# A recurrent attention and a gated MLP on one core: weight signs on GpSimd as f32 words, and a new order of the whole program

## The chip, the core and the metric

The kernel runs on one core of a Trainium2 chip. A core has TensorE (PE, with its weight loads shown as PEld), VectorE (DVE), ScalarE (ACT), GpSimd (POOL) and SyncE (SP), which issues most DMAs. The engines run side by side, each through its own list of instructions in order, and wait for each other by semaphores. SBUF is the working memory of 128 partitions; PSUM, in eight banks, takes what TensorE computes.

The metric is device microseconds of one execution. Before the change the median of three runs is 501.91 us (501.64 to 502.25).

## The reference

For 4 batches, 8 heads, 768 steps and head size 48, a state of 48 x 48 a head is carried along:

```python
for t in range(S):
    cur = np.einsum('bhd,bhe->bhde', u[None] * kt, vt)
    y[:, :, t] = np.einsum('bhd,bhde->bhe', rt, state + cur)
    state = wt[:, :, :, None] * state + np.einsum('bhd,bhe->bhde', kt, vt)
```

The result, as x with 3072 tokens of 384, goes through an MLP with d_ff = 2048:

```python
h = x @ w_in
g = np.where(h >= 1, h, np.where(h <= -1, 0.0, (h + 1) ** 2 / 4))
return g @ w_out
```

The weights come as 64-bit floats, all else as 32-bit ones, and the result is 32-bit.

## The kernel before, in words

**Attention.** The sequence is cut into 12 segments u = 0..11 of 64 steps x 4 batches, 256 tokens each. In a segment VectorE scans w forward and backward (L550 and L545) for the decay products, scales k (L571) and r (L621) with them, and TensorE does the rest in 64 x 64 matmuls: `among` (L591) gives the scores of all pairs of steps, `picked` (L597) keeps the ones that count, `umat` (L660) the segment's own contribution to the state, `crossed` and `along` (L703) the output. k is also transposed (L630). For the first three segments (u < EARLY) the term with u is made by a second `among` on k scaled by u (`with_u`, L561, on ScalarE); later ones make it on VectorE and GpSimd (L609, L611, L614, L617).

**x.** The output y^T of a segment leaves PSUM as an operand x of the MLP, in two parts: a high part rounded for the fast matmul, and the low part that is left (`yevac`, L775 to L781). Each head has 48 rows of 64, so a last quarter of y is spread over the rows that are free: by matmuls with a permutation `perm` in segments 0 and 1 (L800, from a copy at L805), by DMAs from `last` after that. In the last two blocks (FLAT) y goes to `xf` unsplit and is split later, in `divided` (L1150, L1152).

**MLP.** Six blocks of 512 tokens (two segments each) pass 16 slices f of d_ff. `products` does one step (block, slice): nine matmuls into h (L1369), the gate on ScalarE and VectorE (L1178 to L1183), nine matmuls into three accumulators (L1389), two steps behind. Block 0 does slices 0 to 4 of each half alone, and block 1 slices 0 to 13, since a half is one segment and can begin sooner. The last three blocks (FAST) use a scheme with fewer products in the second half (L1045).

**Weights.** Each slice's 768 columns of w_in and w_out come as 64-bit floats, once, and are made into 32-bit ones in `weight(f)`. In order: a DMA into `wraw`; ScalarE takes the upper word with its exponent moved by 2^-112 into `fl` (L481); ScalarE puts the three bits of the lower word that an f32 still holds, as 16-bit numbers, into every other half word of `wraw` (L483); GpSimd, or VectorE for f in SIGNS, puts the sign, a 16-bit 0 or 32768, into the other halves (L485); VectorE shifts `fl` left by three and joins both (L487), so the f32 weight stands in `fl`. ScalarE, or VectorE for f in SPLITS, rounds it into the high part (L477, L475), and VectorE subtracts for the low part (L490). `fl` has three buffers.

**The order.** A planner (`Plan`) writes the order of all engines' instructions by hand. Each `op` has an engine, an estimated cost, a due time, and what it reads and writes; `order` simulates the engines and takes, whenever one is free, the ready operation with the most urgent key. `best` repeats this with keys from `late` (how long before the end an operation must run) and random shakes, and keeps the order with the shortest simulated end. `kept_warm` then puts multiplications of zeros (`zeros`, L439) into gaps of PE, so that its clock stays up.

At the start, SP's loads are ranked: w of both halves, rk of one half, the constants `cst`, rk of the other, weight 0, v, then the rest. `perm` is loaded too.

## Time and profile before

| | |
|---|---|
| median of three runs | 501.91 us (501.64 to 502.25) |
| the profiled execution | 503.06 us; its span, from the first to the last instruction, 501.5 us |
| busy: PE, PEld | 488.0 us (97%), 426.8 us (85%) |
| busy: DVE, ACT, POOL | 404.1 us (81%), 312.7 us (62%), 101.4 us (20%) |
| MLP products, L1369 and L1389 (three groups) | 220.1, 80.3 and 44.5 us of PE |
| zeros, L439 | 13.2 us of PE, all before 40 us |
| weights' signs, L485 on GpSimd | 13 instructions, 41.8 us |
| DMA | 54.30 MB, of it the permutation 192 KB, the constants 98 KB |

A row of a group names line, engine, operation, out<-in, shapes and count, then busy time in us, the mean ns of one, and the idle time of the engine before them with what ended it. A row of the timeline gives start and length in us. The busy time of PE includes the zeros. In the stages' rows the clock is the share of full speed that TensorE was granted.

### The profile page before, as it was taken

The page shows a single profiled execution, that of the slowest core. Times are in us where ns is not written, and L with a number is a line of the kernel's source. Part 1 is how long each engine was busy: PE and PEld are TensorE (multiplying, and loading weights), DVE is VectorE, ACT ScalarE, POOL GpSimd, SP SyncE. Part 2 cuts the span into 40 slices and gives each one's busy share as a digit, 9 for nine tenths or more (in the row PEclk, how much of TensorE's full clock was granted, in tenths as well). Part 3 has the DMA queues.
Part 4 walks back from the last instruction along what each step waited for, and adds up shares of the span by engine and source line. Part 5 has one row for each costly group of instructions (what it writes and reads, how often), then busy time and mean ns, then how long its engine had stood idle before and what let it go on. Part 6 is the DMA issues. An engine that isn't in the chain of part 4 may idle for free.

```text
span 501.5 us, 13736 instructions
## 1 busy us (share of the span) xinstructions
PE 488.0 (97%) x5767; PEld 426.8 (85%) x5767; DVE 404.1 (81%) x702; ACT 312.7 (62%) x658; POOL 101.4 (20%) x80
## 2 busy tenths in 40 slices
PE   6979999999999999999999999999999999999996
PEld 4768988889999998888888788889899989898985
DVE  5899999988888898898999878779877675675573
ACT  4669799855555473765555656788866565465461
POOL 1656604530111111303031124432100000000000
PEclk9989999999999999999999999999999999999999
DMA  8984750522343434446153212222141000010002
GB/s 293 400 300 163 300 211 17 185 81 86 107 133 107 141 103 138 169 137 215 39 210 105 106 52 74 42 52 55 30 118 22 1 1 1 23 41 1 3 1 69
DMA packets 33286, 54.30 MB, mean 108 GB/s; under 512 B 15424, under 2 KB 22720, under 8 KB 33216
## 3 DMA queue, kind: packets, MB, share of 16 engines
q1 hardware_dynamic: 32784, 52.95, 31.9%
q8 instruction: 47, 0.77, 0.6%
q10 hardware_dynamic: 432, 0.39, 0.2%
q14 instruction: 23, 0.19, 0.1%
HBM read 47.04 MB, written 4.72 MB: 103 GB/s over the span
## 4 chain that ended last, share of the span: by engine, by line
PE 90%; DVE 4%; DMA 2%; issue 2%; ACT 1%; SPq 0%; DVEq 0%; ACTq 0%
PE h L1369 39%; PE acc L1389 20%; PE acc L1045 10%; PE bank L1045 9%; PE bank L703 4%; PE bank L591 3%; PE bank L630 2%; PE bank L660 1%; DMA cst<-in_consts 1%; DMA rk<-in_rk 1%; DVE fl L487 1%; PE bank L439 1%; PE acc L591 1%; DVE wt L490 1%; DVE y L545 0%
## 5 line engine op out<-in xcount | busy, mean ns | idle before, releaser
L1369 PE MATMUL h<-x,wt 128*128 128x512 f32 (+1 forms) x1035 | 220.1, 360 | 3.0 <-DVE x L779 2.9
L1369 PEld LDWEIGHTS h<-x,wt 128*128 128x128 f32 x1035 | 169.5, 189 | 31.7 <-DVE x L779 3.1
L1389 PE MATMUL acc<-gh,wt 128*128 128x256 f32 (+1 forms) x402 | 80.3, 335 | 0.0
L1389 PEld LDWEIGHTS acc<-gh,wt 128*128 128x128 f32 x402 | 60.9, 188 | 7.4
L1007 DVE SCALAR_TENSOR_TENSOR rk<-rk,h 128x512 f32<-128x512 f32 x48 | 32.8, 683 | 35.8 <-ACT rk L1006 34.2
L1178 ACT ACTIVATE g<-h 128x256 f32<-128x256 f32 (+1 forms) x67 | 31.9, 476 | 44.8 <-PE h L1369 40.6
L1004 ACT ACTIVATE rk<-h 128x512 f32<-128x512 f32 x48 | 28.6, 596 | 38.8 <-PE h L1369 38.8
L485 POOL TENSOR_SCALAR wraw<-fl 128x768 uint16<-128x768 f32 x13 | 41.8, 3224 | 51.4 <-ACT wraw L483 49.9
L1180 DVE SCALAR_TENSOR_TENSOR g<-g,h 128x256 f32<-128x256 f32 (+1 forms) x67 | 35.2, 529 | 14.4 <-ACT g L1179 12.4
L1389 PE MATMUL acc<-gl,wt 128*128 128x256 f32 (+1 forms) x201 | 44.5, 329 | 0.0
L1182 ACT CAST gh<-g 128x256 fp32r<-128x256 f32 (+1 forms) x67 | 32.7, 494 | 18.8 <-DVE g L1180 8.8
L617 POOL TENSOR_TENSOR r<-cst,d 128x512 f32<-128x512 f32 x18 | 20.2, 1143 | 99.8 <-PE bank L703 81.7
L1183 DVE TENSOR_TENSOR gl<-g,gh 128x256 fp32r<-128x256 f32 (+1 forms) x67 | 38.7, 589 | 0.8 <-ACT gh L1182 0.7
L1389 PEld LDWEIGHTS acc<-gl,wt 128*128 128x128 f32 x201 | 32.3, 188 | 4.0
L1179 ACT ACTIVATE g<-g 128x256 f32<-128x256 f32 (+1 forms) x67 | 34.4, 513 | 1.1
L550 DVE TENSOR_TENSOR_SCAN p<-wq,seeds 128x520 f32<-128x520 f32 x24 | 32.0, 1331 | 3.2 <-DMA wq<-in_w 2.3
L1006 ACT ACTIVATE rk<-rk 128x512 f32<-128x512 f32 x48 | 30.4, 634 | 0.9
L545 DVE TENSOR_TENSOR_SCAN y<-wq,seeds 128x520 f32<-128x520 f32 x24 | 29.8, 1242 | 0.8
L609 POOL TENSOR_TENSOR nk<-nk 128x768 f32<-128x768 f32 x9 | 17.3, 1920 | 61.4 <-DMA nk<-in_nk 37.9
L1013 DVE TENSOR_TENSOR gl<-rk,gh 128x512 fp32r<-128x512 f32 x36 | 25.5, 717 | 2.7 <-ACT gh L1012 2.4
L1013 DVE TENSOR_TENSOR g_again<-rk,nk_again 128x512 fp32r<-128x512 f32 x33 | 22.8, 701 | 5.8 <-ACT nk_again L1012 5.5
L1012 ACT CAST gh<-rk 128x512 fp32r<-128x512 f32 x36 | 22.1, 619 | 8.3 <-DVE rk L1007 4.7
(212 smaller groups left out, 914.5 us busy)
## 6 DMA issues: line engine op xcount, KB each, us to landing
rk<-in_rk SPq DMA_DIRECT2D x24, 512.0 KB, 5.3
wraw<-in_wbits SPq DMA_DIRECT2D x16, 768.0 KB, 7.5
nk<-in_nk SPq DMA_DIRECT2D x9, 768.0 KB, 4.7
wq<-in_w SPq DMA_DIRECT2D x24, 260.5 KB, 2.9
vn<-in_v SPq DMA_DIRECT2D x12, 384.0 KB, 6.8
last<-in_w SPq DMA_DIRECT2D x12, 256.0 KB, 3.0
out_y<-xf SPq DMA_DIRECT2D x15, 128.0 KB, 1.8
out_y<-g SPq DMA_DIRECT2D x6, 256.0 KB, 2.2
```

The source lines that it names most:

```text
L485: op(on, 0.62 if f in SIGNS else 3.2, due, [("fl", k)], [("raw", f)], lambda: e.tensor_scalar(out=half(1), in0=s, scalar1=0.0, scalar2=327 ...
L550: V.tensor_tensor_scan(out=pv[:, q].rearrange("p n c -> p (n c)"), data0=w[:, 0:SEG], data1=sv, initial=0.0, op0=ALU.mult, op1=ALU.add,)
L1007: op("DVE", 0.66, due, [("h", n)], [qk], lambda: V.scalar_tensor_tensor(out=gf, in0=gf, scalar=1.0, in1=bank[plan.given[hk]], op0=ALU.min, ...
L1013: op("DVE", 0.67, due, [key, ("h", i, k)], fresh_in(("l", i, k)), lambda: V.tensor_tensor(out=spare(k, 3 + i), in0=x, in1=spare(k, i).bitc ...
L1045: PE.matmul(bank[i][:, half * UT : half * UT + UT], lhsT=w[wi], rhs=g[gi], start=(b, i) not in opened, stop=True, skip_group_check=True)
L1178: op("ACT", c, due, [("h", n)], [("g", gk)], lambda: nc.scalar.activation(gs, hs(), AF.Relu, scale=0.5, bias=0.5), uses=[hk])
L1179: op("ACT", c, due, (), [("g", gk)], lambda: nc.scalar.activation(gs, gs, AF.Square))
L1180: op("DVE", 0.13 + 0.53 * k, due, [("h", n)], [("g", gk)], lambda: nc.vector.scalar_tensor_tensor(out=gs, in0=gs, scalar=1.0, in1=hs(), op ...
L1182: op("ACT", c, due, [("g", gk)], [("gh", gk)], lambda: nc.scalar.copy(ghs, gs))
L1183: op("DVE", 0.17 + 0.54 * k, due, [("g", gk), ("gh", gk)], [("gl", gk)], lambda: nc.vector.tensor_tensor(out=gls, in0=gs, in1=ghs.bitcast( ...
L1369: nc.tensor.matmul(hp, lhsT=wx[f][:, cs], rhs=xt[:, j, :], start=n == 0, stop=n == 8)
L1389: nc.tensor.matmul(o[j], lhsT=wx[f][:, cs], rhs=gt, start=first and i == 0, stop=stop and i == 2, skip_group_check=True)
```

## The change

**Weights.** `xf[0]`, the unsplit x of even blocks, holds two tiles z of 768 words until block 2 needs it. GpSimd multiplies `fl` by 0.0 into z for every slice: what is left is a word with only the sign. ScalarE writes the low bits into the lower half of each word of z, and VectorE joins z with the shifted `fl`. SIGNS is gone, SPLITS is empty. For f of 4 and more, GpSimd copies the high part in ScalarE's place (SPARED); for the first four ScalarE does it. The copies of y into x of block 2 write z's names too, so that they wait for the last weight.

**x.** FLAT holds blocks 1 to 5 (it was 4 and 5): y of these is copied unsplit into `xf`, and `divided` splits it, for blocks 1 to 3 planned right behind their second segment.

**Start.** rk of both halves comes ahead of the constants; u stands in two new columns of w, so that `with_u` no longer reads `cst`; `perm` is made on GpSimd by a fill and three copies, and is no longer loaded; u's broadcast (`u_sb`) is loaded after weight 5.

**Planner.** It models PE's instruction stream in blocks of 256 with edges and fetch times, a price for the switch between small and wide matmuls, and holds PE up to 0.25 us for another small operation after a small one. Costs of PE's small operations are lower, the zeros' cost per column is higher (fewer columns in a gap). There are 12 shakes in place of 40, and then 19 listed moves, each of which shifts keys near one time. The result is another order of the whole program.

```diff
-FLAT = {NB - 2, NB - 1}
+FLAT = set(range(1, NB))
 
 WARM = 12
 
 SCRATCH = 2048
 
-USE, SPAN, COLUMN = 0.68, 3.4, 0.00168
+USE, SPAN, COLUMN = 0.68, 3.4, 0.00184
 
 EAGER, LATE = 16.0, 0.3
-RISES = 7.0
-COLD = 7.0
+RISES = COLD = 6.0
 
 LANES = 8
 
-BACK, SHAKES, SHAKE, SEED = 4, 40, 0.7, 5
+BACK, SHAKES, SHAKE, SEED = 4, 12, 0.7, 3
+
+MOVES = (521500, 587009, 625859, 75142, 354096, 937336, 551989, 701578, 29685, 79344, 78778, 524362, 665920, 756794, 334125, 534668, 621384, 343240, 480776)
...
-    BLOCK, FETCH = 256, 3.9
+    BLOCK, EDGE, LEAD, DENSE = 256, 194, 3, 1 / 700
+    FETCH, BUSY, SLOWER = 3.75, 45.0, 5.0
+    SWITCH, HOLD, LOOK = 0.125, 0.25, 30.0
+    EVENT = 0.00025
+    RATES, WAY = ((8.0, 300e3), (60.0, 390e3), (1e9, 280e3)), 2.1
...
+        for move in MOVES:
+            self.nudge(move)
...
+    def attempt(self, keys):
+
+        for op, key in zip(self.ops, keys):
+            op["key"] = key - self.LOOK * op["look"]
+        order = self.order()
+        if order is None:
+            return False
+        for _ in range(3):
+            was, self.put_in = self.put_in, self.idle(order)
+            self.replay(order)
+            if {n: x[-1] for n, x in was.items()} == {n: x[-1] for n, x in self.put_in.items()}:
+                break
+        end = max(self.end.values())
+        if self.found is None or end < self.found[0]:
+            self.found = end, order, (self.begin, self.end, self.given, self.extra, self.put_in, keys)
+            return True
+        self.put_in = self.found[2][-2]
+        return False
...
+    def nudge(self, move):
+
+        self.back()
+        draw = random.Random(move)
+        keys = self.late() if draw.random() < 0.1 else list(self.keys)
+        at, wide, much = draw.uniform(0.0, self.found[0]), draw.choice((4.0, 10.0, 25.0)), draw.choice((0.3, 1.0, 3.0, 8.0))
+        for n in range(len(keys)):
+            if abs(self.begin[n] - at) < wide:
+                keys[n] += draw.gauss(0.0, much)
+        return self.attempt(keys)
...
+    def pe_takes(self, n, t, pe, between=0.0):
+
+        op = self.ops[n]
+        idle = self.records(n)
+        was = pe["small"] and not idle
+        cost = op["cost"] + self.SWITCH * (op["small"] != was) + self.EVENT * op["code"]
+        for code, start, span in ((idle, between, t - between), (op["code"] * (1 + self.DENSE), t, cost)):
+            past = -(pe["count"] - self.EDGE) % self.BLOCK
+            if past < code:
+                at = start + span * past / code
+                when = pe["edge"] + (self.SLOWER if at < self.BUSY else self.FETCH)
+                if start == t:
+                    cost += max(0.0, when - at)
+                pe["edge"] = max(at, when)
+            pe["count"] += code
+        pe["small"] = op["small"]
+        return cost
...
+            if e == "PE" and pe["small"] and forced.get(e) is None:
+                n = min((n for n in open_[e] if ops[n]["small"] and ready(n) <= t + self.HOLD), key=lambda n: (ready(n), n), default=None)
+                if n is not None:
+                    t = max(t, ready(n))
...
-SPLITS = {2, 7}
-SIGNS = {9, 10, 12}
+SPLITS = set()
+SPARED = set(range(4, NF))
+SIGN, HALF = 1.0, 1.08
...
-    xf = tiles(len(FLAT), [128, 3, WIDE], F32, "xf")
+    xf = tiles(2, [128, 3, WIDE], F32, "xf")
...
-        def front():
-
-            return wraw[f].rearrange("p c two -> p (c two)")[:, 0:768]
-
-        def half(i):
-            return front().bitcast(U16).rearrange("p (c two) -> p c two", two=2)[:, :, i]
+        z = xf[0].rearrange("p a b -> p (a b)")[:, 768 * (f % 2) : 768 * (f % 2) + 768]
+        zk = ("z", f % 2)
+
+        def low_half():
+            return z.bitcast(U16).rearrange("p (c two) -> p c two", two=2)[:, :, 0]
 
...
-            if f in SPLITS:
+            if f in SPARED:
+                G.tensor_copy(w_hi[f], s)
+            elif f in SPLITS:
                 V.tensor_copy(w_hi[f], s)
             else:
                 A.copy(w_hi[f], s)
...
-        op("ACT", 1.09, due, (), [("raw", f)], lambda: A.activation(half(0), words(0, U32), AF.Copy, scale=LOW))
-        on, e = ("DVE", V) if f in SIGNS else ("POOL", G)
-        op(on, 0.62 if f in SIGNS else 3.2, due, [("fl", k)], [("raw", f)], lambda: e.tensor_scalar(
-            out=half(1), in0=s, scalar1=0.0, scalar2=32768.0, op0=ALU.is_lt, op1=ALU.mult))
-        op("DVE", 0.97, due, [("raw", f), ("flight", f % FLIGHT)], [("fl", k)], lambda: V.scalar_tensor_tensor(
-            out=s.bitcast(I32), in0=s.bitcast(I32), scalar=3, in1=front(), op0=ALU.logical_shift_left, op1=ALU.bitwise_or), port=True)
-        op(*(("DVE", 0.48) if f in SPLITS else ("ACT", 0.83)), due, [("fl", k)], [("wh", f), ("raw", f)], split, port=f in SPLITS)
+        op("POOL", SIGN, due, [("fl", k)], [zk], lambda: G.tensor_scalar(out=z, in0=s, scalar1=0.0, scalar2=None, op0=ALU.mult))
+        op("ACT", 1.09, due, [("raw", f), ("flight", f % FLIGHT)], [zk], lambda: A.activation(low_half(), words(0, U32), AF.Copy, scale=LOW))
+        op("DVE", 0.97, due, [zk], [("fl", k)], lambda: V.scalar_tensor_tensor(
+            out=s.bitcast(I32), in0=s.bitcast(I32), scalar=3, in1=z.bitcast(I32), op0=ALU.logical_shift_left, op1=ALU.bitwise_or), port=True)
+        op(*(("POOL", HALF) if f in SPARED else ("DVE", 0.48) if f in SPLITS else ("ACT", 0.83)), due, [("fl", k)], [("wh", f), ("raw", f)], split, port=f in SPLITS and f not in SPARED)
...
-            load(due, wq[slot[q]], a["w"][u, q], [("w", slot[q])], first=rank(1 - q))
-            load(due, rk[slot[q]], a["rk"][u, q], [("k", slot[q]), ("r", slot[q])], first=rank(4 - 2 * q))
+            s = slot[q]
+            load(due, wq[s], a["w"][u, q], [("w", s)], first=rank(1 - q))
+            load(due, rk[s], a["rk"][u, q], [("k", s), ("r", s)], first=rank(3 - q))
         if u == 0:
-            load(due, cst, a["consts"], ["cst"], first=3)
+            load(due, cst, a["consts"], ["cst"], first=4)
...
-            load(due, perm, a["perm"], ["perm"], [vk])
+            op("POOL", 0.4, due, [], ["perm"], lambda: G.memset(perm, 0.0))
+            for j in range(3):
+                def shifted(x, lo):
+                    return x.rearrange("p (h c) -> p h c", h=2)[:, :, lo : lo + 16]
+                op("POOL", 0.2, due, ["cst"], ["perm"], lambda j=j: G.tensor_copy(
+                    shifted(perm[:, 128 * j : 128 * j + 128], D), shifted(ident, 16 * j)))
...
-                A.mul(ku[:, q, cs], rk[slot[q]][:, 1, cs], u_col[:, 2 * q + pr : 2 * q + pr + 1])
+                A.mul(ku[:, q, cs], rk[slot[q]][:, 1, cs], wq[slot[q]][:, SEG + 1 + pr : SEG + 2 + pr])
...
-                op("ACT", 1.0, due, [("k", s), "cst"], [("ku", q), "nk"], lambda q=q: with_u(q))
+                op("ACT", 1.0, due, [("k", s), ("w", s)], [("ku", q), "nk"], lambda q=q: with_u(q))
...
-                op("ACT", 0.27 if what else 0.48, due, [("b", by[g])], [names(what, 0, g)], lambda g=g, w=what: yevac(g, 0, w))
+                op("ACT", 0.27 if what else 0.48, due, [("b", by[g])], [names(what, 0, g)] + [("z", i) for i in range(2) if blk == 2], lambda g=g, w=what: yevac(g, 0, w))
...
+                if u % 2 and u // 2 in FLAT and u // 2 < NB - 2:
+                    divided(u // 2)
...
-            if b + 1 in FLAT:
+            if b + 1 in FLAT and b + 1 >= NB - 2:
...
-    wz = np.pad(wz.reshape(NU, 2, 2, D, SEG), [(0, 0)] * 4 + [(0, 1)])
+    wz = np.pad(wz.reshape(NU, 2, 2, D, SEG), [(0, 0)] * 4 + [(0, 3)])
+    wz[..., SEG + 1 :] = u.reshape(2, 2, 2, D).transpose(0, 2, 3, 1)
```

More of the change, by code (lines that the diff above doesn't have):

```diff
@@ L86, in __init__, with add @@
         self.given, self.extra = {}, {}
-    def add(self, engine, cost, emit, due, reads=(), writes=(), port=False, size=0, fresh=True, first=None, grab=False, uses=(), drop=None, code=0):
+    def add(self, engine, cost, emit, due, reads=(), writes=(), port=False, size=0, fresh=True, first=None, grab=False, uses=(), drop=None, code=0, small=False, look=False):
         deps = {self.writer[x] for x in (*reads, *writes) if x in self.writer}
@@ new lines, in replay @@
+    def replay(self, order):
+        ops = self.ops
+        free, end, begin, lands = {}, {}, {}, []
+        port = bus = 0.0
+        pe = dict(count=self.LEAD, edge=-99.0, small=False)
+        for n in order:
+            op = ops[n]
+            e = op["e"]
+            t = max((end[m] + self.after(m, n) for m in op["deps"]), default=0.0)
+            if n in self.extra:
+                t = max(t, end[self.extra[n]] + self.HOPS[ops[self.extra[n]]["e"]])
+            t = max(t, free.get(e, 0.0))
+            if op["port"]:
+                t = max(t, port)
+            if op["size"] and len(lands) >= LANES:
+                t = max(t, lands[-LANES])
+            cost = op["cost"]
+            if e == "PE":
+                cost = self.pe_takes(n, t, pe, free.get(e, 0.0)) * (2 if t < RISES else 1)
+            begin[n], end[n] = t, t + cost
+            free[e] = end[n] - self.OVERLAP.get(e, 0.0)
+            if op["port"]:
+                port = free[e]
+            if op["size"]:
+                bus, end[n] = self.lands(bus, t, op["size"])
+                lands.append(end[n])
+        self.begin, self.end = begin, end
@@ L233, in order @@
         forced, given, extra = {}, {}, {}
[L234 to L241 removed]
+        pe = dict(count=self.LEAD, edge=-99.0, small=False)
         spare = [(0.0, b, None) for b in SPARE]
@@ L249, in ready @@
                 t = max(t, min(spare)[0]) if spare else never
-            if ops[n]["code"] > 64:
-                t = max(t, fetched(ops[n]["code"]) - ops[n]["cost"])
+            if ops[n]["small"]:
+                past = -(pe["count"] + self.records(n) - self.EDGE) % self.BLOCK
+                m, took = n, 0.0
+                while m is not None:
+                    code = ops[m]["code"] * (1 + self.DENSE)
+                    if past < code:
+                        when = pe["edge"] + (self.SLOWER if t < self.BUSY else self.FETCH)
+                        return max(t, when - took - ops[m]["cost"] * past / code)
+                    past, took, m = past - code, took + ops[m]["cost"], ops[m]["then"]
             return t
```

159 lines of the change are left out of this document (79 added, 80 removed).

## The prediction

> **What bounds the kernel now.** I read the page's head first, then the busy time by stage, then the chain of waits in the stage that loses time.
>
> ```profile
> span 501.5 us, 13736 instructions
> PE 488.0 (97%) x5767; PEld 426.8 (85%) x5767; DVE 404.1 (81%) x702; ACT 312.7 (62%) x658; POOL 101.4 (20%) x80
> ```
>
> ```profile
> 9.50:29.50 20.00, 17.00 (x312) 13.05 (x312) 17.86 (x26) 13.45 (x24) 10.79 (x4) 0.91 1.04 399
> ...
> 105.00:310.00 205.00, 205.00 (x3230) 178.16 (x3229) 178.14 (x318) 115.45 (x287) 40.08 (x33) 1.00 0.37 122
> 310.00:496.50 186.50, 186.10 (x1190) 167.62 (x1188) 131.48 (x243) 118.38 (x224) 15.48 (x20) 1.00 0.12 29
> ```
>
> The columns are the stretch, then busy time and count of PE, PEld, DVE, ACT and POOL, then the granted clock, DMA share and GB/s. TensorE is the bound: 97% of the span, and 205.00 of 205.00 us from 105 to 310, with 0.4 us missing in the 186.5 after that. The head of the kernel is different: PE counts as busy there for 17 of 20 us, but much of that work is not wanted by anyone. Its rows between the end of the first segment's attention and the first product say so:
>
> ```profile
> 18.96 1.11 PE L703 MATMUL bank<-r,vn 64*48 64x64 f32 x64
> 20.01 2.61 PE L439 MATMUL bank<-zero 128*128 128x512 f32 x8
> 22.45 1.53 PE L800 MATMUL bank<-ob,nk 128*128 128x128 f32 x12
> 23.82 2.25 PE L439 MATMUL bank<-zero 128*128 128x512 f32 x8
> ...
> 29.46 1.21 PE L1369 MATMUL h<-x,wt 128*128 128x256 f32 x8 [2.90 <-DVE x L779]
> 30.60 1.89 PE L591 MATMUL bank<-rk,nk 64*64 64x64 f32 x64
> ```
>
> L439 multiplies zeros to hold the clock. From 20.07 to 29.46 us, 9.39 us, PE does 1.53 us of work that counts (the spreading, L800) apart from a single matmul. The chain of waits tells what it waits for:
>
> ```profile
> 2.36 5.36 DMA cst<-in_consts
> ...
> 7.81 0.92 ACT nk L561 x2
> ...
> 13.31 1.53 PE bank L439 x6
> ...
> 26.93 0.94 DVE fl L487
> 27.87 0.47 DVE x L779
> 28.34 0.60 DVE rk L571
> 28.93 0.48 DVE x L779
> ```
>
> So x, the operand of the first product, is late because VectorE decodes a weight (L487) and scales another segment's k (L571) between and ahead of the two halves of x (L779). ScalarE does the same one step earlier: the copies that feed L800 wait behind a weight.
>
> ```profile
> 21.64 0.27 ACT L805 COPY ob<-bank 128x128 f32<-128x128 f32 x1
> 21.79 1.10 ACT L483 ACTIVATE wraw<-wraw 128x768 uint16<-128x768 uint32 x1
> 22.74 0.26 ACT L805 COPY ob<-bank 128x128 f32<-128x128 f32 x1
> 24.48 0.47 ACT L781 CAST x<-bank 128x384 fp32r<-128x384 f32 x1
> 25.66 0.46 ACT L781 CAST x<-bank 128x384 fp32r<-128x384 f32 x1
> ```
>
> The last instruction's chain runs on PE from there, so a microsecond won before 29.46 us is kept to the end, if the engines that feed PE can follow.
>
> **The change, part by part.** *What x needs.* Its own work after 20.07 us is two copies (0.27 + 0.26), the spreading (1.53), two casts (0.47 + 0.46), two subtractions (0.47 + 0.48), 3.94 us; five changes of engine at some 0.05 us, as between the chain's rows 28.93 + 0.48 and 29.46, make 4.2. Of 9.39 us, 5.2 are other work standing in the way. Ahead of it the change gives more: the scaling by u (L561) no longer waits for the constants, which landed at 7.72 us, but reads u beside w; that and the later fillers (1.53 us at 13.31) I take at 0.5, 0 to 2. The head can thus win 5.7 us, and 7.2 at most.
>
> *What the weights need.* The sign moves:
>
> ```profile
> L485 POOL TENSOR_SCALAR wraw<-fl 128x768 uint16<-128x768 f32 x13 | 41.8, 3224 | 51.4 <-ACT wraw L483 49.9
> L485 DVE TENSOR_SCALAR wraw<-fl 128x768 uint16<-128x768 f32 x3 | 1.8, 616 | 0.0
> L475 DVE CAST wt<-fl 128x768 fp32r<-128x768 f32 x2 | 1.1, 546 | 0.0
> L477 ACT CAST wt<-fl 128x768 fp32r<-128x768 f32 x14 | 11.7, 833 | 3.1 <-DVE fl L487 3.1
> L429 POOL MEMSET r<- 128x512 f32 x2 | 1.0, 524 | 0.0
> L609 POOL TENSOR_TENSOR nk<-nk 128x768 f32<-128x768 f32 x9 | 17.3, 1920 | 61.4 <-DMA nk<-in_nk 37.9
> ```
>
> A GpSimd operation with one f32 input of 768 and an f32 output isn't in the trace. It lies between a fill (524 ns for 512, so 0.79 us) and the product of two inputs (1.92 us). With one input it is nearer to the fill: I take 1.1 us, and 1.2 for the copy into the high part, which rounds as well. Were both as slow as the 16-bit sign, 3.2 us, POOL would need 6.4 us a weight. At 1.1 the time from a weight's landing to its low part falls by 2.1 us, as the 1.09 us of ScalarE's low half keeps its length and only changes places with the sign. Twelve copies leave ScalarE (12 x 0.83 = 10 us), and the copies of weights 2 and 7 leave VectorE; the one of weight 2 goes to ScalarE. None of that is PE time by itself: it is cover for the work around x.
>
> *What VectorE can follow.* This sets how much of 5.7 us is kept, since VectorE is nearly full:
>
> ```profile
> 17.30:60.00 42.70, 39.26 (x770) 34.37 (x771) 41.26 (x66) 32.29 (x69) 25.73 (x9) 0.96 0.74 270
> 60.00:105.00 45.00, 45.00 (x402) 37.59 (x401) 42.17 (x63) 38.09 (x66) 15.57 (x6) 1.00 0.39 140
> ```
>
> Its idle time up to 105 us, where block 1 begins, is 1.44 + 2.83 = 4.27 us. Removed from it: three signs, 1.85 us; two casts, 1.09; and for segment 2 the low parts of x taken from PSUM, by
>
> ```profile
> L779 DVE TENSOR_TENSOR x<-bank,x 128x384 fp32r<-128x384 f32 x14 | 7.5, 549 | 2.0 <-ACT last L781 1.9
> L779 DVE TENSOR_TENSOR last<-bank,last 128x128 fp32r<-128x128 f32 x12 | 3.1, 281 | 1.4 <-ACT x L781 0.8 <-ACT last L781 0.7
> ```
>
> two of 0.55 and two of 0.28 against one subtraction of 0.95 later, 0.7 us. That is 7.9 us of room. [...]
>
> ```profile
> 14.99 6.44 POOL L485 TENSOR_SCALAR wraw<-fl 128x768 uint16<-128x768 f32 x2 [11.93 <-ACT wraw L483]
> 18.54 1.51 DVE L487 SCALAR_TENSOR_TENSOR fl<-fl,wraw 128x768 int32<-128x768 int32 x1
> 22.78 0.93 DVE L487 SCALAR_TENSOR_TENSOR fl<-fl,wraw 128x768 int32<-128x768 int32 x1
> 205.55 1.83 POOL L609 TENSOR_TENSOR nk<-nk 128x768 f32<-128x768 f32 x1 [10.73 <-PE acc L1389]
> 205.82 2.11 DVE L571 TENSOR_TENSOR rk<-rk,y 128x512 f32<-128x512 f32 x1
> ```
>
> Beside the old sign L487 took 1.51 us in place of 0.93, 0.58 lost; beside L609 the scaling L571, elsewhere 0.68, took 2.11 and ended when GpSimd had. GpSimd's operations on weights go from 13 to 28 (16 signs, 12 copies). If an operation costs VectorE 0.29 us on average (every second one hits, for 0.58), the 15 more cost 4.3 us, and the room is 3.6 us. At the lower bound no new one hits: the room is 7.9 and the head's 5.7 come whole. At the upper bound each of the 28 costs 0.58, 16.2 us against 3.8 before (13 x 0.29): 12.4 us more, 4.5 beyond the room. I take 0.29, nearest to L485's own rows, and so **3.6 us** from the head; the range keeps −4.5 to 7.2.
>
> [...]
>
> *Order.* Costs, hold rules and moves of the planner only reorder; PE's work stays. Each return from 64-wide matmuls to wide ones has a price:
>
> ```profile
> 135.78 1.05 PE h L1369 x9
> ...
> 138.38 1.25 PE h L1369 x9
> ```
>
> 0.20 us. Segments 2 to 10 have some four each; letting small operations follow each other may save one in ten to one in three. I take 4 x 0.2 = **0.8 us**, 0 to 2.5. [...]
>
> *Costing nothing.* The identity pieces of perm are built by GpSimd while it idles (11.93 us before 14.99) and replace a load. z lies in the tile of x for block 2, whose evacuation now waits for the last weight: PE wants that weight within block 0, before 105 us, and sixteen steps of block 1 lie between, each 4.2 us by the row 135.78 (1.05 us for half of one product of two), so some 60 us cover it. The tile of block 5 waits for block 3's splitting; behind that would queue ScalarE's copies of segment 10, and PE's banks behind them, but block 3's last segment is 7, three segments earlier. The copies and subtractions of blocks 1 to 3 run where VectorE is at 87 to 94% or less. GpSimd's copy waits in order ahead of the next sign; it holds that by VectorE's 0.93 us at most, while a weight is wanted once in 4.2.
>
> Sum: 3.6 + 0.8 = 4.4 us. The profiled execution took 503.06 us, 1.56 around its span; 503.06 − 4.4 = 498.7. The shown runs' median is 1.15 lower, 501.91, so **497.5 us**.
>
> **The rivals.** *First, the head wins whole* and GpSimd's short operations cost VectorE no more than the long ones did: 5.7 to 7.2 and up to 2.5 from the order, 492 to 495.5. For it speaks that GpSimd's time on weights falls by 10 us (41.8 against 16 x 1.1 + 12 x 1.2 = 32), against it VectorE's 42.17 of 45 us busy.
>
> *Second, slower:* the port. Each new GpSimd operation blocks VectorE for half its 1.1 us or more, all 28 of them, between 15 and 105 us; room falls from 7.9 to −4.5 us, x and the weights come when VectorE lets them, and PE has zeros or nothing to do before 105 us. 501.91 + 4.5 − 0.8, about 505.6; it decides once a GpSimd operation costs VectorE over (7.9 + 3.8) / 28 = 0.42 us. For it speaks 205.82; against it that only half of the 3 us signs hit anything.
>
> *Third, nothing moves:* the new order puts other work where the old stood, or loads decide. The DMA share is 1.04 from 9.5 to 29.5 us, so weights 3 and later come no sooner. Then 501 to 502.8. *Fourth, the change doesn't do what it says*: the f32 sign is no shorter than the 16-bit one; 6.4 us a weight against PE's 4.2 makes PE starve for the last ten weights, over 510.
>
> **How the numbers follow.** Forecast (495.5 to 500.8) 0.55; first rival 0.18; second 0.14; third 0.10; fourth 0.03. What a measurement tells from no change is 0.2%, 1 us. Faster: 0.55 + 0.18 + 0.03 of the third, 0.76; same: 0.07 of the third and 0.01 of the second's light end, 0.08; slower: 0.13 + 0.03, 0.16. For 8 in 10 I leave out the lower end of the first rival and the upper half of the second: 492.0 to 503.0; the likeliest case alone is 495.5 to 500.8.
>
> **What would show it.** In the new profile: POOL's two groups on weights at 1.0 to 1.3 us; the first product of nine matmuls at 23 to 26 us in place of 29.46, with less of L439 ahead; PE without waits after 40 us; VectorE's L487 group at a mean near 1.0 us (second rival: over 1.2). Wrong would make it: a first product as late as now, or one that is early with PE idle or on zeros between 30 and 60 us.

## The result, and the profile after

The changed kernel takes 508.0 us (median; 507.5 to 508.5) against 502.1 us (501.6 to 502.3) of the kernel before: 1.011 times as long, 95% interval 1.009 to 1.014. It is 5.9 us slower, where 4.4 us faster was forecast.

The profiled execution took 507.52 us. Lines are now those of the changed kernel: the first product of the MLP is L1484 (it was L1369), x comes from L893 (L779), the zeros are L549 (L439), the sign on GpSimd L593, ScalarE's low half L594, VectorE's join L595 (L487) and low part L598 (L490), and GpSimd's copy into the high part L583. The page's head, the shares of the chain that ended last by engine, and the groups of the sign and of the low half:

```profile
span 505.8 us, 13661 instructions
PE 483.6 (96%) x5751; PEld 423.2 (84%) x5751; DVE 400.8 (79%) x679; ACT 312.2 (62%) x654; POOL 116.0 (23%) x99
...
PE 78%; DVE 5%; POOL 5%; ACT 4%; issue 4%; DMA 2%; SPq 1%; DVEq 0%; POOLq 0%; ACTq 0%
...
L593 POOL TENSOR_SCALAR xf<-fl 128x768 f32<-128x768 f32 x16 | 41.3, 2586 | 24.6 <-ACT fl L591 19.8
...
L594 ACT ACTIVATE xf<-wraw 128x768 uint16<-128x768 uint32 x16 | 17.4, 1086 | 18.6 <-POOL xf L593 18.5
```

Span and profiled time rose by 4.3 and 4.5 us; the rest of the 5.9 is that the profiled execution before took 503.06 us, 1.0 above its median, and the one after 507.52, 0.5 below its own. PE has 4.4 us *less* busy time than before (its zeros fell from 13.2 to 8.3 us), so nothing was added to it: it waits more. The sign takes 2586 ns on average, and ScalarE stands idle for 18.5 us because of it. The chain says the same: PE has 78% of it, where it had 90% before, and GpSimd, which was not on it, has 5%. The shares before were

```profile
PE 90%; DVE 4%; DMA 2%; issue 2%; ACT 1%; SPq 0%; DVEq 0%; ACTq 0%
```

Where PE lost time is in the stretches, first before, then after (columns as in the prediction):

```profile
20.00:30.00 10.00, 7.00 (x40) 4.71 (x34) 9.82 (x16) 7.95 (x15) 6.28 (x3) 1.00 1.01 388
30.00:40.00 10.00, 9.65 (x168) 8.07 (x166) 9.02 (x15) 6.81 (x14) 5.17 (x2) 0.83 0.59 203
...
90.00:110.00 20.00, 20.00 (x176) 16.09 (x175) 18.38 (x29) 14.51 (x26) 7.76 (x4) 1.00 0.38 123
```

```profile
20.00:30.00 10.00, 8.29 (x153) 6.74 (x144) 8.97 (x14) 8.15 (x17) 4.13 (x3) 1.00 0.91 353
30.00:40.00 10.00, 5.89 (x93) 3.98 (x95) 7.54 (x13) 6.33 (x12) 4.52 (x4) 1.00 0.74 264
...
90.00:110.00 20.00, 17.90 (x75) 13.58 (x74) 18.00 (x25) 12.31 (x20) 9.17 (x7) 1.00 0.07 20
110.00:240.00 130.00, 129.11 (x2044) 116.84 (x2046) 111.34 (x198) 76.29 (x193) 26.90 (x18) 1.00 0.41 133
```

From 20 to 30 us PE does more than before (153 matmuls against 40), from 30 to 40 less (93 against 168), and it has gaps from 90 to 110, where before it had none. VectorE is *less* busy in the first two stretches (16.5 us against 18.8), so it wasn't short of time there.

Counting only matmuls that are wanted, each at its usual length (0.117 us for 256 columns, 0.0165 for the 64-wide ones), and taking their sum from the time elapsed, gives PE's lost time up to each moment. It is worked out from all of PE's rows, and holds to some tenths of a us:

| lost up to (us) | 30 | 40 | 110 | 240 | 490 |
|---|---|---|---|---|---|
| before | 23.0 | 27.4 | 28.5 | 31.3 | 35.1 |
| after | 20.4 | 27.4 | 33.2 | 37.0 | 39.2 |

So the head was won by 2.6 us, all of it was given back within the next 10 us, another 4.7 were lost up to 110 us, and little happened later. What PE waited for between 20 and 130 us, before (three columns: total, times, longest) and after:

```profile
PE h L1369 <- DVE x L779: 2.9, 1, 2.9
PE bank L736 <- ACT kt L639: 0.2, 1, 0.2
```

```profile
PE bank L744 <- DVE r L711: 4.1, 3, 2.3
PE h L1484 <- DVE g L1294: 2.1, 3, 1.0
PE bank L914 <- ACT ob L919: 1.4, 1, 1.4
```

The timeline of the changed kernel shows how one of the 2.3 us came about; each row has its start, its length, and in brackets what its engine waited for:

```profile
32.91 2.59 POOL L593 TENSOR_SCALAR xf<-fl 128x768 f32<-128x768 f32 x1 [1.93 <-ACT fl L591]
...
35.53 1.06 ACT L594 ACTIVATE xf<-wraw 128x768 uint16<-128x768 uint32 x1 [2.40 <-POOL xf L593]
...
36.62 0.96 DVE L595 SCALAR_TENSOR_TENSOR fl<-fl,xf 128x768 int32<-128x768 int32 x1 [2.46 <-ACT xf L594]
...
37.50 1.36 DVE L711 COPY_PREDICATED r<-below,bank 128x512 f32<-128x512 int32 x2
...
38.28 0.66 PE L744 MATMUL bank<-cst,rk 128*128 128x128 f32 x4 [2.30 <-DVE r L711]
```

GpSimd makes a sign in 2.59 us. ScalarE has the low half as its next instruction, so all of ScalarE waits 2.40 us; VectorE has the join as its next, and waits 2.46 us; behind the join stands L711, the choice of pairs of steps for the attention, which has nothing to do with weights, and TensorE waits for that.

### The profile page after: what moved, and what is told of

The parts are those of the page before. It is cut to its first block, busy times and chain, and to the rows that moved or that the text cites. A ratio compares the mean times of both kernels' runs of the same rounds, so it can differ in the third digit from the quotient of the medians.

```text
span 505.8 us, 13661 instructions
## 1 busy us (share of the span) xinstructions
PE 483.6 (96%) x5751; PEld 423.2 (84%) x5751; DVE 400.8 (79%) x679; ACT 312.2 (62%) x654; POOL 116.0 (23%) x99
## 4 chain that ended last, share of the span: by engine, by line
PE 78%; DVE 5%; POOL 5%; ACT 4%; issue 4%; DMA 2%; SPq 1%; DVEq 0%; POOLq 0%; ACTq 0%
PE h L1484 34%; PE acc L1504 15%; PE acc L1159 10%; PE bank L1159 9%; POOL xf L593 5%; PE bank L817 4%; PE bank L705 2%; PE bank L744 2%; PE bank L774 1%; DVE wt L598 1%; DMA rk<-in_rk 1%; DVE gl L1297 1%; ACT xf L594 1%; ACT fl L591 1%; DMA xf<-last 1%
## 5 line engine op out<-in xcount | busy, mean ns | idle before, releaser
L1484 PE MATMUL h<-x,wt 128*128 128x512 f32 (+1 forms) x1035 | 218.6, 360 | 2.8 <-DVE g L1294 2.1
L1484 PEld LDWEIGHTS h<-x,wt 128*128 128x128 f32 x1035 | 167.5, 188 | 33.1 <-issue 2.2
L731 POOL TENSOR_TENSOR r<-cst,d 128x512 f32<-128x512 f32 x18 | 21.8, 1232 | 111.3 <-PE bank L817 58.3
L593 POOL TENSOR_SCALAR xf<-fl 128x768 f32<-128x768 f32 x16 | 41.3, 2586 | 24.6 <-ACT fl L591 19.8
L1297 DVE TENSOR_TENSOR gl<-g,gh 128x256 fp32r<-128x256 f32 (+1 forms) x67 | 40.6, 616 | 2.2 <-ACT gh L1296 2.2
L659 DVE TENSOR_TENSOR_SCAN y<-wq,seeds 128x520 f32<-128x520 f32 x24 | 31.2, 1298 | 0.8
L594 ACT ACTIVATE xf<-wraw 128x768 uint16<-128x768 uint32 x16 | 17.4, 1086 | 18.6 <-POOL xf L593 18.5
L1126 ACT CAST gh<-rk 128x512 fp32r<-128x512 f32 x36 | 22.2, 618 | 9.2 <-DVE rk L1121 5.8
```

What stands on the lines that cost most here:

```text
L593: op("POOL", SIGN, due, [("fl", k)], [zk], lambda: G.tensor_scalar(out=z, in0=s, scalar1=0.0, scalar2=None, op0=ALU.mult))
L659: V.tensor_tensor_scan(out=y_[:, ::-1], data0=w[:, SEG:0:-1], data1=sv[:, ::-1], initial=0.0, op0=ALU.mult, op1=ALU.add)
L1297: op("DVE", 0.17 + 0.54 * k, due, [("g", gk), ("gh", gk)], [("gl", gk)], lambda: nc.vector.tensor_tensor(out=gls, in0=gs, in1=ghs.bitcast( ...
L1484: nc.tensor.matmul(hp, lhsT=wx[f][:, cs], rhs=xt[:, j, :], start=n == 0, stop=n == 8)
```

## The experiments

Three theories went into them. *Price*: the sign, forecast and planned at about 1.1 us, takes 2.6. *Port*: GpSimd's reading beside VectorE slows VectorE (a name alone: no run shows what the two would share). *Order*: the new order and start are the worse ones. Later the price was split into the sign's *length behind the wait for the upper words* (chain) and its reading (port). Ratios are against the kernel before, on the same chip, with 95% intervals; the diffs give the changed lines in short. "VectorE's loss" is, for all VectorE instructions between 15 and 110 us that overlap one of GpSimd, what they took above the median of their form by more than 0.1 us: 4.2 us before, 9.0 after.

**The sign as a copy, and as a fill.** One operation is exchanged, all orders stay. In both the sign is left out.

```diff
-lambda: G.tensor_scalar(out=z, in0=s, scalar1=0.0, scalar2=None, op0=ALU.mult)
+lambda: G.tensor_copy(z, s)        # e1
+lambda: G.memset(z, 0.0)           # e2
```

> The changed kernel in its own order, with GpSimd's sign (2.6 us) replaced by a plain copy of the same 768 words, which takes 0.83 us where the trace has one: about the 1.0 us that the planner counts. The sign is left out, so the weights are wrong. Theory 1, the price (the order was planned for a sign of 1.0 us and meets one of 2.6): 496 to 500 us, ScalarE's 18.5 us of waits for the sign nearly gone. Theory 2, the port (28 GpSimd instructions that read SBUF hold up VectorE): their number and kind stay, 504 to 508. Theory 3, the order itself (it is worse whatever the sign costs): 506 to 509.

> As the run with the copy, but the sign is replaced by a fill of 768 words (some 0.8 us), which reads nothing; the sign is left out. Price: within 1 us of the run with the copy. Port: 12 reading GpSimd instructions are left of 28, so 3 to 4 us below the run with the copy. Order: 506 to 509.

The copy took 1162 ns at the median (827 at the least): 501.2 us, 0.999 (0.997 to 1.001). The fill took 738 ns: 498.8 us, 0.993 (0.990 to 0.996). So the whole loss goes away with this one operation, and with a copy as long as the prediction had taken for the sign the change is worth nothing: the true price accounts for 6.8 of the 10.5 us between 497.5 and 508.0. e1 lies 1.2 us above what the price theory had named, and e2 2.4 us below e1, between what price (1 at most) and port (3 to 4) had named. The waits for the sign, in e1:

```profile
ACT xf L594 <- POOL xf L593: 3.3, 6, 0.9
```

in e2:

```profile
ACT xf L594 <- POOL xf L593: 0.3, 1, 0.3
```

**Which form costs what.** The sign in four forms, by the slice's number modulo four: a product with a number, a product with a tile of zeros, a comparison, a copy (the last two leave the sign out of their slices).

```diff
+ f % 4 == 0:  G.tensor_scalar(out=z, in0=s, scalar1=0.0, scalar2=None, op0=ALU.mult)
+ f % 4 == 1:  G.tensor_tensor(out=z, in0=s, in1=zero (repeated), op=ALU.mult)
+ f % 4 == 2:  G.tensor_scalar(out=z, in0=s, scalar1=0.0, scalar2=None, op0=ALU.is_lt)
+ f % 4 == 3:  G.tensor_copy(z, s)
```

> The order of the changed kernel with four forms of the GpSimd sign side by side, by the slice's number modulo four: a product with the number zero (as in the changed kernel), a product with a tile of zeros, a comparison with zero written as a 32-bit word, and a plain copy; the last two leave the sign out of their slices, and this run is for the durations alone. Price theory, if it is the operation with a number that is slow on this engine: 2.1 us or more for the first and the third, 1.6 to 1.9 us for the second (three operands), 0.83 us for the fourth. If it is the 32-bit type or the stage instead, all four are alike.

From the views of the four lines, ns at the least, median and most:

```profile
L574 POOL TENSOR_SCALAR xf<-fl x4: 2133/2503/2952, 11.5 to 81.0; 128x768 f32<-128x768 f32 x4
L576 POOL TENSOR_TENSOR xf<-fl,zero x4: 1824/2428/2762, 17.7 to 86.2; 128x768 f32<-128x768 f32 x4
L579 POOL TENSOR_SCALAR xf<-fl x4: 2303/2842/2850, 19.5 to 90.4; 128x768 f32<-128x768 f32 x4
L581 POOL COPY xf<-fl x4: 828/1718/1842, 28.2 to 98.3; 128x768 f32<-128x768 f32 x4
```

One execution took 506.5 us, with a mixture of signs. The least values are taken for the undisturbed ones. By them the same tile, type and count take 0.83 us copied and 2.13 us multiplied by a number on this engine; the product of *two* tiles is shorter, 1.82. So it is the operation with a number that is dear, not the type.

**The truth told to the planner.**

```diff
-SIGN, HALF = 1.0, 1.08
+SIGN, HALF = 2.6, 0.85
```

> The changed kernel, planned anew with the measured costs on GpSimd: sign 2.6 us in place of 1.0, copy 0.85 in place of 1.08. Nothing else differs. Price: the planner routes around the long sign, 499 to 504. Port: the same 28 instructions, 505 to 508. Order: 505 to 509.

507.6 us, 1.011 (1.008 to 1.014): no better. But it is another loss. ScalarE's wait for the sign is down to 0.3 us, and lost time up to 110 us is 29.5 us, 1.0 above before; then it rises to 38.5 by 240 us. Of these 9.0 us 4.4 lie between 220 and 240; PE's stretch and its rows there:

```profile
220.00:240.00 20.00, 17.95 (x310) 0.91 0.45 145
```

```profile
222.93 1.11 PE L817 MATMUL bank<-r,vn 64*64 64x64 f32 x63
225.92 0.27 PE L817 MATMUL bank<-r,vn 64*64 64x64 f32 x1 [1.88 <-issue]
226.11 2.21 PE L1484 MATMUL h<-x,wt 128*128 128x512 f32 x7
```

PE stops before the last of 64 small matmuls, waiting for nothing that the profile shows (where such stops stand is told in the last section), and the clock granted in the stretch is 0.91. So a newly found order can lose several us at another place, and only runs that keep the changed kernel's order (e1, e2, e7, e9, e13, e14, e15, e17) can be compared finely.

**How far the order alone moves the time.** Another start of the planner's draws:

```diff
-BACK, SHAKES, SHAKE, SEED = 4, 12, 0.7, 3
+BACK, SHAKES, SHAKE, SEED = 4, 12, 0.7, 5
```

> The changed kernel with another start of the planner's draws (5 instead of 3) and nothing else: every cost and every instruction is the same, only the order found differs. It measures how far the order alone moves the time. If the order that was sent along fits the chip by its own luck, 509 to 513 us; if the planner's orders are all alike, 507 to 509 us; if that order is a bad draw, 504 to 506 us.

510.4 us, 1.016 (1.011 to 1.021): 2.4 us above the changed kernel. The order sent along is no bad draw, as far as one other draw can tell; whether it is a lucky one, as the range that came true has it, one draw doesn't show.

**One part at a time.** e4 puts the old decode back into the changed kernel (16-bit signs, on GpSimd for 13 slices; high parts on ScalarE and VectorE). e5 puts the new decode into the kernel before, with its planner and start. e10 is e5 with the sign as a fill, so without signs.

```diff
# e4: the changed kernel with
-SPLITS, SPARED = set(), set(range(4, NF)); z in the tile of x, sign as an f32 word
+SPLITS, SIGNS = {2, 7}, {9, 10, 12}; the decode of the kernel before, planned at 3.2 us
# e5: the kernel before with
+SPLITS, SPARED, SIGN, HALF = set(), set(range(4, NF)), 1.0, 1.08; the decode of the changed kernel
# e10: e5 with
-G.tensor_scalar(out=z, in0=s, scalar1=0.0, scalar2=None, op0=ALU.mult)
+G.memset(z, 0.0)
```

> The changed kernel with the weights decoded as before (16-bit signs of 3.2 us on 13 slices, planned at 3.2), all else of the change kept and planned anew. Price: all costs are true, so the new planner's gains at the start show, 496 to 501. Port: 13 instructions as before, 499 to 502. Order: 505 to 509.

> The new decode of the weights alone, on the kernel before: its planner, its loads and its heads stay, only the sign on GpSimd as a 32-bit word, the low half written over it and the high parts of thirteen slices on GpSimd come in; the planner counts 1.0 us for a sign and 1.08 for a high part, as in the changed kernel. Price and port theory (the decode is what loses): the old decode in the new order stood at 504.8 against 508.0 with the new one, 3.2 us; so here 501.8 + 3 = 505 us, with TensorE waiting between 30 and 110 us. Order theory (the new planner and the earlier start make the loss, and the decode is nearly neutral): 501 to 503 us.

> The new decode alone on the kernel before (508.9 us) with its own order kept, and the sign on GpSimd replaced by one fill of 0.74 us; the sign is left out. Price and port theory: the sign is what made that kernel slow, so it falls by as much as the changed kernel fell with a fill (508.0 to 498.8, 9 us): 499 to 501 us. If the rest of the new decode (the tile that waits for x, the high parts on GpSimd) costs something of its own: 503 to 506 us.

e4: 504.8 us, 1.006 (1.004 to 1.009). e5: 508.9 us, 1.013 (1.010 to 1.016). e10: 499.9 us, 0.995 (0.993 to 0.997). So the new decode alone makes the whole loss, on the old planner too, and with a fill in the sign's place it gains there nearly what it gains on the new one (0.995 against 0.993, the intervals overlap). In e5 the waits are those of the changed kernel:

```profile
ACT xf L486 <- POOL xf L485: 18.7, 13, 2.5
...
DVE fl L487 <- ACT xf L486: 4.8, 3, 2.7
```

The new planner and start bring nothing that these runs resolve with the new decode, and with the old one they lose 3 us; e4 missed what price and port had named (502 at most) and came within 0.2 us of the order theory's 505. Its order is a new draw, so that this is the planner itself is not shown, and it stays open.

**The sign on another engine.**

```diff
# e6, planned at 0.92 us, high part at 0.85
+op("ACT", SIGN, due, [("raw", f)], [zk], lambda: A.activation(z, words(1, F32), AF.Copy, scale=0.0))
# e8, planned at 0.55 us, high part at 0.85
+op("DVE", SIGN, due, [("fl", k)], [zk], lambda: V.tensor_scalar(out=z, in0=s, scalar1=0.0, ..., op0=ALU.mult), port=True)
# e11: even slices as e8; odd ones as below, planned at 1.9 us; high parts on GpSimd for even slices alone
+op("POOL", 1.9, due, [("fl", k)], [zk], lambda: G.tensor_tensor(out=z, in0=s, in1=zero (repeated), op=ALU.mult))
```

> The changed kernel with the sign made by ScalarE (a scaled copy by zero out of the upper words as they came in), planned at 0.92 us, the high parts still on GpSimd, planned at 0.85. Price theory: no GpSimd instruction stands ahead of the weights' low half any more, so the loss between 30 and 110 us goes and the time is 499 to 502 us, as with the sign replaced by a GpSimd copy (501.2) or a fill (498.8); ScalarE gets 14.7 us more in that stretch. Port theory: 13 instead of 29 reading GpSimd instructions, so VectorE's loss beside GpSimd falls from 9.0 us to about 4 and the time is at the lower end, 499. Order theory: what the old decode showed in the new order stays, 504 to 505 us.

> The changed kernel with the sign made by VectorE (the same product by zero, planned at 0.55 us), the high parts still on GpSimd, planned at 0.85. It gives VectorE 16 x 0.55 = 8.8 us more of its own, and takes 16 GpSimd instructions from beside it. Price theory: the two nearly cancel against the sign by a GpSimd copy, 500 to 503 us. Port theory: the GpSimd instructions that are gone had cost VectorE some 5 us of the 9.0, so about 502. Order theory: 504 to 506 us.

> The changed kernel with the sign of the even slices on VectorE (0.55 us) and of the odd ones on GpSimd as a product with a tile of zeros, planned at 1.9 us; high parts on GpSimd for the even slices from the fourth on alone, planned at 0.85, the others on ScalarE. GpSimd then has some 2 us for each slice instead of 3.6, and all prices are planned near what was measured. Price and port theory: most of the loss goes, 500 to 503 us, a little better or worse by the order found. Order theory: 504 to 506 us, as with the old decode in the new order.

504.1 us (single executions from 500.1 to 506.1), 509.1 and 515.4 us; 1.003 (1.000 to 1.005), 1.013 (1.009 to 1.016), 1.026 (1.020 to 1.032). In e6 the signs of the weights are lost. All three have orders of their own: their lost time from 110 to 240 us is 4.8, 6.7 and 8.6 us, against 2.8 before, so their ends don't tell the theories apart. Up to 110 us e6 and e8 lose 29.5 and 30.9, between before (28.5) and after (33.2): another engine for the sign, in an order of its own, takes away a part of the early loss. e8 and e11 lie above all that was named for them, and e6 at the order theory's 504. e11 lost 35.8 by then; its odd slices' sign took up to 5.6 us, and I have no cause for that.

**Length, wait and reading, crossed.** A fill does two things less than the sign: it does not read, and it does not wait for `fl`. All four keep the order, and leave the sign out.

```diff
# e9: three fills, no wait, no read
+[G.memset(z, 0.0) for _ in range(3)]
# e13: a copy of one column, which waits for fl, and three fills
+[G.tensor_copy(z[:, 0:1], s[:, 0:1])] + [G.memset(z, 0.0) for _ in range(3)]
# e15: the same with one fill
+[G.tensor_copy(z[:, 0:1], s[:, 0:1]), G.memset(z, 0.0)]
# e14: the product, of a constant tile: it reads, but doesn't wait
+G.tensor_scalar(out=z, in0=zero (repeated), scalar1=0.0, scalar2=None, op0=ALU.mult)
```

> The order of the changed kernel, with the sign on GpSimd replaced by three fills of the same tile with zeros in a row, 3 x 0.74 = 2.2 us: as long as the true sign at its shortest (2.13 us), but without a read. The sign is left out, so the output has none. Length theory (the low half waits for the sign, and it matters alone how long that takes): 506 to 508 us, near the changed kernel's 508.0. Port theory (what hurts is that GpSimd reads beside VectorE): 499 to 502 us, as with one fill (498.8), and VectorE's loss beside GpSimd between 15 and 110 us at about 6 instead of 9 us.

> The order of the changed kernel; the sign is replaced by a copy of one column of the upper words, which makes GpSimd wait for them as the sign did, and three fills behind it, together 2.3 us. The sign is left out. Chain theory (the low half, the join and the product stand behind the sign, and the sign behind the upper words, so its length counts in full): 505 to 508 us, near the changed kernel's 508.0. Port theory (GpSimd's reading slows VectorE): 499 to 501 us, as with the three fills that wait for nothing (499.5).

> As the one before, but with one fill behind the copy of one column, together 0.85 us; the sign is left out. Against the sign as a GpSimd copy (501.2 us, 0.83 us undisturbed, waits and reads): chain theory, the same or a little less, 500 to 501 us; port theory: as with the fill that waits for nothing, 498.8 us.

> The order of the changed kernel; the sign is replaced by the same product by zero, but of a constant tile of zeros, so that it has the length (2.13 us or more) and reads, but waits for no upper words. The sign is left out. Chain theory: 499 to 501 us, as with the three fills that wait for nothing. Port theory: 505 to 508 us, and VectorE's loss beside GpSimd between 15 and 110 us near the changed kernel's 9.0 us.

| | sign, median us | waits for `fl` | reads 768 | ScalarE waits for it, us | VectorE waits for the low half, us | VectorE's loss, us | us | ratio (95%) |
|---|---|---|---|---|---|---|---|---|
| e2 | 0.74 | no | no | 0.3 | 0 | 6.3 | 498.8 | 0.993 (0.990 to 0.996) |
| e15 | 1.41 | yes | no | 3.6 | 0.5 | 5.9 | 498.3 | 0.993 (0.991 to 0.995) |
| e9 | 2.21 | no | no | 8.3 | 0.8 | 2.8 | 499.5 | 0.995 (0.992 to 0.997) |
| e1 | 1.16 | yes | yes | 3.3 | 0 | 10.7 | 501.2 | 0.999 (0.997 to 1.001) |
| e14 | 2.45 | no | yes | 11.2 | 1.0 | 9.5 | 505.6 | 1.007 (1.003 to 1.010) |
| changed | 2.63 | yes | yes | 18.5 | 4.3 | 9.0 | 508.0 | 1.011 (1.009 to 1.014) |
| e13 | 2.45 | yes | no | 22.2 | 7.9 | 3.1 | 512.2 | 1.020 (1.015 to 1.024) |

The two rows that decide come from e13's waits up to 110 us:

```profile
ACT xf L594 <- POOL xf L593: 22.2, 14, 2.5
...
DVE fl L595 <- ACT xf L594: 7.9, 6, 2.7
```

e13 hardly disturbs VectorE (3.1 us, less than before the change), and is the slowest. So a long sign behind the wait is enough for the whole loss: the *chain*. Against e15, the two more fills, 1.48 us on GpSimd a weight, cost 13.8 us; without the wait (e9 against e2) they cost 0.7. Behind the wait, 1.4 us still costs nothing.

Not all of the 13.8 us is waiting. The clock granted in e13 fell early:

```profile
20.00:30.00 10.00, 7.21 (x94) 5.80 (x91) 7.40 (x13) 6.48 (x13) 3.61 (x6) 0.83 0.89 342
...
40.00:60.00 20.00, 18.88 (x299) 17.42 (x300) 16.52 (x29) 15.84 (x37) 12.12 (x17) 0.83 0.50 177
```

That is at most 0.17 x 30 = 5.1 us. e9, e14 and e15 have 1.00 from 20 to 60 us; the changed kernel has 0.92 from 40 to 60, at most 1.6 us. Without these e13 would stand at some 507 us and the changed kernel at some 506, an estimate. Whether PE's waits brought the clock down was not tested.

Reading has a price beside it, seen best between e15 and e1, where the sign is no longer: 2.9 us. VectorE's two groups on weights say the same, in e15:

```profile
L598 DVE TENSOR_TENSOR wt<-fl,wt 128x768 fp32r<-128x768 f32 x16 | 16.0, 1002 | 0.0
L595 DVE SCALAR_TENSOR_TENSOR fl<-fl,xf 128x768 int32<-128x768 int32 x16 | 15.8, 990 | 0.8 <-ACT xf L594 0.5
```

and in e1:

```profile
L598 DVE TENSOR_TENSOR wt<-fl,wt 128x768 fp32r<-128x768 f32 x16 | 17.8, 1117 | 0.0
L595 DVE SCALAR_TENSOR_TENSOR fl<-fl,xf 128x768 int32<-128x768 int32 x16 | 17.0, 1064 | 0.0
```

(115 + 74) ns x 16 = 3.0 us. e14, the long sign that reads and doesn't wait for `fl`, came where the port theory had it (505 to 508 us, VectorE's loss near 9.0), not the chain theory (499 to 501): 6.1 us above e9, with 6.7 us more of VectorE's loss. It does not isolate the reading: its sign is longer than e9's as well, ScalarE still waits 11.2 us for it, and its executions lie between 503.3 and 507.5 us. Chain and reading don't add up: the changed kernel has both and is faster than e13. Of the others e9 and e15 came where the port theory had them too, and e13 above the chain theory's 508, 11 us and more from the port theory's. So neither theory holds alone, and either makes most of the loss with a sign of this length. That the sign makes it is shown (e1, e2, e10); how the 9 us divide between waiting and reading stays open.

**Ways out.** e16 takes the sign from the words as they landed, so that it needn't wait for ScalarE; e17 keeps the order and makes half of the sign on GpSimd and half on VectorE, as a 16-bit comparison before the join; e18 is e17 with its prices planned. All three make the whole sign.

```diff
# e16, planned at 2.2 us, high part at 0.85
+op("POOL", SIGN, due, [("raw", f)], [zk], lambda: G.tensor_scalar(out=z, in0=words(1, F32), scalar1=0.0, ..., op0=ALU.mult))
# e17, e18
+G.tensor_scalar(out=z[:, 0:384], in0=s[:, 0:384], scalar1=0.0, scalar2=None, op0=ALU.mult)
+V.tensor_scalar(out=upper half words of z[:, 384:768], in0=s[:, 384:768], scalar1=0.0, scalar2=32768.0, op0=ALU.is_lt, op1=ALU.mult)
# e18: the planner's prices
+SIGN, HALF, JOIN = 1.1, 0.85, 1.32
```

> The changed kernel with the sign taken from the upper words as they landed instead of from ScalarE's copy of them, so that it can start 0.9 us and more before; planned at 2.2 us, the high parts at 0.85. Nothing of the computation is left out. Chain theory: much of the loss goes, 500 to 503 us. Port theory: the reads stay, 505 to 508 us. Another order than the changed kernel's, so 2 us either way are its own.

> The order of the changed kernel; GpSimd makes the sign of the first 384 columns of a weight alone (half of 2.13 us, 1.1 us), and VectorE that of the other 384 as a 16-bit comparison just before the join (some 0.35 us, 5.6 us over 16 weights). Nothing of the computation is left out. Chain theory: the chain is at the length that the prediction had taken, as with the sign as a GpSimd copy (501.2 us), and VectorE's 5.6 us come partly on top: 501 to 504 us. Port theory: 28 GpSimd instructions still read, so 504 to 508 us.

> The same halves, but with the planner told 1.1 us for the sign, 0.85 for the high part and 1.32 for the comparison and the join together, so that it finds another order. Chain theory: 499 to 503 us, at best below the kernel before. Order theory (a new order is some 2 us worse or better by its own luck, as between 508.0 and 510.4 us with another start of the draws): 501 to 506 us.

509.9 us, 1.016 (1.012 to 1.019); 504.9 us, 1.007 (1.004 to 1.009); 511.3 us, 1.019 (1.016 to 1.021). e17 in the changed kernel's order is 3.1 us faster than it, with ScalarE's wait for the sign down from 18.5 to 5.3 us, and 3.7 slower than e1, in the range of the port theory; its half sign took 1347 ns at the median (1171 at the least). e16 has VectorE's loss at 12.9 us, the highest of the kernels that make the whole sign, and like e18 loses time from 110 to 240 us in its new order: 8.2 and 7.2 us. Both took longer than either theory had named. No kernel that makes the sign was as fast as the kernel before.

## Why the prediction was wrong

**The step that failed** is the price of "a GpSimd operation with one f32 input of 768 and an f32 output": taken at 1.1 us as "nearer to the fill", it is 2.13 us at the least and 2.63 at the median. It lay above the bound of 1.92 us that the prediction had from the trace for the whole of it; only the 16-bit sign, 3.2 us, which it named as a case, would have held it. The copy next to it was taken too dear: 1.2 us, measured 0.99 on average and 0.82 at the least. With 2.6 us, the time from a weight's landing to its low part falls by 0.6 us, not by the 2.1 that were counted on.

**What a longer sign would do was priced wrongly too.** The prediction saw it as GpSimd's throughput: 6.4 us a weight against PE's 4.2, in the fourth rival. It came to 2.59 + 0.99 = 3.6 us a weight, below 4.2, and GpSimd was busy for 8.7 of the 20 us from 20 to 40 and 14.0 of those from 40 to 60. The waits show latency in its place. Before, the sign came behind the low half, ScalarE never waited for it, and VectorE hardly, although it was longer; up to 110 us all waits for it were

```profile
DVE fl L487 <- POOL wraw L485: 1.3, 2, 0.9
```

Now the sign stands ahead of the low half, so that ScalarE waits for it as well (18.5 us) and VectorE behind ScalarE (4.3 us), each with its next, unrelated instructions behind. That the low half "only changes places with the sign" was costed at nothing, and this is where the order of the two counts. At 1.4 us it cost nothing (e15, 498.3 us against 498.8 in e2). How much the sign's reading adds stays open (e14).

**The head.** Right in kind; PE's rows after:

```profile
24.92 0.60 PE L549 MATMUL bank<-zero 128*128 128x256 f32 x2
25.65 0.39 PE L1484 MATMUL h<-x,wt 128*128 128x256 f32 x1
26.25 1.92 PE L1484 MATMUL h<-x,wt 128*128 128x256 f32 x14 [0.21 <-DVE x L893]
```

The first product began at 25.65 us, within the 23 to 26 that were named, and zeros from 20 to 30 us fell from 4.9 to 2.5 us. The gain was 2.6 us of lost time at 30 us, not 5.7, and it was spent at 40. With the sign as a fill the gain at 40 us is 3.9 us (27.4 against 23.5), the copy's is 2.7. Up to 1.7 us of either is the granted clock, 0.83 from 30 to 40 us before and 1.00 in e1 and e2.

**VectorE and the port.** The 4.3 us more came near for the changed kernel (9.0 against 4.2, 4.8 more), by luck, since the sign there is 2.6 us long. For the forecast's own case, a sign of 1.1 us that reads, e1 shows 10.7, so 6.5 more: the term was 2.2 us too low there, and e1's 501.2 in place of 497.5 is in part this. The second rival did not come: it asked for a mean over 1.2 us, and the groups after are

```profile
L598 DVE TENSOR_TENSOR wt<-fl,wt 128x768 fp32r<-128x768 f32 x16 | 18.1, 1139 | 0.7 <-POOL wt L583 0.7
L595 DVE SCALAR_TENSOR_TENSOR fl<-fl,xf 128x768 int32<-128x768 int32 x16 | 16.7, 1044 | 4.4 <-ACT xf L594 4.3
L583 POOL CAST wt<-fl 128x768 fp32r<-128x768 f32 x12 | 11.8, 987 | 10.0 <-DVE fl L595 6.8 <-ACT gh L1296 3.3
```

Its *place* was right, VectorE late between 15 and 105 us, but in the main as a wait for the low half, not as blocked instructions.

Nor was every new GpSimd operation such a block, as that rival had it. The joins at 21.16, 46.12 and 61.56 us lay wholly within a sign and took 0.94 to 0.96 us, the median of all joins being 0.95; others took 0.3 or 0.6 longer. Beside GpSimd's copy VectorE did come out late: the three instructions on weights that began within one, at 73.02, 81.72 and 93.31 us, took 1.57 to 1.58 us and ended 0.81 us after it. And the prediction misread its row at 205.82: by it L571 ended at 207.93, 0.55 us after GpSimd's 207.38, as one of 0.68 that began only then nearly would.

**GpSimd's copy in order ahead of the next sign** was to hold it by 0.93 us at most. It waited 6.8 us in four times for the join, up to 2.2 us: the join itself was late.

**The order's 0.8 us** cannot be seen: the lost time after 110 us is 6.0 us in the changed kernel and 6.6 before, and one draw of the planner differs from another by 2.4 us.

**The test that was named** spoke: the first product early, and PE idle between 30 and 60 us (4.1 us of the first ten). With a stand-in for the sign that is short enough and doesn't read, the sum nearly holds: 498.3 us (e15) against 497.5. That is the total alone, since the head's 5.7 us and the order's 0.8 don't show.

## What to carry to other kernels

Before an operation is moved to an engine where the trace shows only other operations, take its price from the dearest of its kin, not from the nearest in inputs: here a fill, a copy, a product of two and a product with a number lie between 0.74 us (e2) and 2.13 us (e7, at the least). When a step is moved ahead of another engine's step, count who queues behind each waiting instruction; a wait of 2.4 us reached TensorE through two engines whose other work had nothing to do with it. And test such a suspicion crosswise, with something as long that neither reads nor waits, since a fill takes away three things at once.

## What the runs showed of the hardware that was not expected

- GpSimd multiplied 128 x 768 f32 numbers by a number in 2.13 us, by a tile in 1.82, and copied them in 0.83 (e7, at the least); it filled them in 0.74 (e2, median). With half the columns the product with a number took 1.17 us (e17, at the least).
- A copy on ScalarE with scale zero left no sign: in e6 the signs of the weights are lost, and its result is as far off as that of e14, which leaves the sign out (relative error 34.81 in both). VectorE and GpSimd kept the sign in their product by zero (e8, the changed kernel). The reason is not shown.
- PE stood for 1.88 us before the last of 64 small matmuls, waiting for nothing that the profile shows (e3). In the 20 traces there are 19 such stops of 0.3 us and more behind 15 us and before a wanted matmul, and at each PE's count of instructions, its few semaphore instructions among them, is 193 or 194 above a multiple of 256 (6594 in e3, 1217 at 39.9 us in e14, 449 at 17.49 us in the changed kernel, a stop of 0.56 us). Through that count the order set, in these traces, which work they hit. The changed planner counts with such places (`BLOCK, EDGE = 256, 194`); what happens there no trace shows.
